# Low parts of six input weight blocks in the first tile: made on VectorE, or by ScalarE and an accumulating DMA

## The chip, the cores and the metric

The kernel runs on one core of a Trainium2 chip. The metric is the device time of one execution in microseconds (us), the median of several runs. Five engines have instruction streams of their own: TensorE (PE; PEld are its weight loads), VectorE (DVE), ScalarE (ACT), GpSimd (POOL) and SyncE (SP, which only issues DMAs). They meet at semaphores, and within one engine the instructions go in the order of the program.

## The reference, cut to what matters

Inputs are float32. Attention in chunks of 64 gives `x` (4608 tokens by 512), and two feed-forward layers follow:

```
h = x @ w_in                      # 512 -> 2048
x = (h * cos(h)) @ w_out          # 2048 -> 512
a, b = x @ w1, x @ w2             # 512 -> 1024 each
out = ((a * b) @ w3) @ w_out2     # 1024 -> 1024 -> 512
```

## The kernel before, in words

**Two-part products.** TensorE multiplies a rounded format (`fp32r`). To keep float32 accuracy every operand is held as a high part (the value rounded to `fp32r`) and a low part (the value minus its high part). `mm3` (lines 111 to 113) makes each product as three matmuls: high x high, weight high x data low, and, on line 113, weight low x data high. So line 113 is the first to read a weight's low part.

**Tiles and groups.** The tokens go in 9 tiles of 512. For each tile the first layer is done in groups of two blocks of `w_in` (blocks `in 2g` and `in 2g+1`, each 128 x 512) and two of `w_out`. Groups 0 to 4 of every tile come first, the others in a second pass. In the first tile a group's work on TensorE is: `stepP` (24 matmuls for one half of the group's hidden values, the first 12 with block `in 2g`, the next 12 with `in 2g+1`), a piece of attention for the next tile, `stepQ` (24 matmuls for the other half), then `x2_mm` of the group before (24 matmuls into `acc`), and more attention. Between them ScalarE and VectorE form `h * cos(h)`.

**Conversion of weights.** The weights come in as 64-bit words and are turned into float32 on the chip, in the first tile, while it is computed. `conv_tick` moves a pipeline by one block: `conv_c` makes the high part `w` of the oldest block (ScalarE, line 189), `conv_b` finishes the next block's float32 value `cw` (VectorE, line 144) and, for an input block, stores it to DRAM, `conv_a` starts the one after (ScalarE line 136, VectorE lines 137 and 138), and then the low part of the oldest block is made. Twenty blocks go through, in the order in 0, in 1, out 0, out 1, in 2, in 3, out 2, ... A hand-written string of letters per group sets the order of all work, and a `v` in it is one tick; there are four in a group, so that each group converts the two output blocks of its own and the two input blocks of the next group. The input blocks are the last two ticks, shortly ahead of the group that reads them.

**Two ways to a low part.** For the input blocks and the output blocks 0 and 1 it is one VectorE subtraction (line 215). For the output blocks 2 to 9 ScalarE writes the negative of the value's rounded part into the low half (line 212), and a DMA that GpSimd issues (line 213) adds the float32 value to it. Those blocks are read by `x2_mm` only, in the next group.

**Where `cw` lives.** A rotating set of three buffers, except for every second of the output blocks 2 to 9, which have halves of weight slot 24.

Of the kernel before, what the change touches and what calls it, by code (L numbers as in the profile page):

```python
# [12 lines left out]
U32 = mybir.dt.uint32  # L13
# [4 lines left out]
P = 128  # L18
NT = 4608
TT = 512  # L20
# [37 lines left out]
def chunk_attention_two_ffn(  # L58
# [15 lines left out]
    wpool = ctx.enter_context(tc.tile_pool(name="wpool", bufs=1))  # L74
# [26 lines left out]
    def f32(ap):  # L101
        return ap.bitcast(F32)
# [10 lines left out]
        nc.tensor.matmul(ps, a[1], b[0], start=False, stop=last)  # L113


    W, raws, halfway, more = {}, {}, {}, []
    src = {"in": w_in, "out": w_out, "w1": w1, "w2": w2, "wo2": wo2, "w3": w3t}

    def load_w(key):
        n = cq.index(key) if key in cq else 0  # L120
        t = (wpool.tile([P, TT, 2], U32, tag=f"w{20 + n % 5}", name="raw") if n >= 5 and n % 5 < 2
             else wk.tile([P, TT, 2], U32, tag="stage", name="raw", bufs=3))
        nc.sync.dma_start(out=t, in_=src[key[0]][key[1]].bitcast(U32).rearrange("p (t w) -> p t w", w=2))
        raws[key] = t

    def conv_a(key):

        raw = raws[key]
        lo, hi = raw[:, :, 0], raw[:, :, 1]
        if key[0] == "out" and key[1] > 1 and key[1] % 2 == 0:  # L130
            if not more:
                more.append(wpool.tile([P, 2, TT], U32, tag=f"w{NSLOT - 1}", name="cw2"))
            m = more[0][:, key[1] // 2 % 2]
        else:
            m = wk.tile([P, TT], U32, tag="cw", name="cw", bufs=3)
        nc.scalar.activation(lo.bitcast(I32), lo, AF.Copy, scale=2.0 ** -29)
        nc.vector.tensor_scalar(m, hi, 3, 0x3FFFFFFF, op0=ALU.logical_shift_left, op1=ALU.bitwise_and)
        nc.vector.scalar_tensor_tensor(m, hi, 0xC0000000, m, op0=ALU.bitwise_and, op1=ALU.bitwise_or)
        halfway[key] = m

    def conv_b(key):

        m = halfway[key].bitcast(I32)
        nc.vector.tensor_tensor(out=m, in0=m, in1=raws.pop(key)[:, :, 0].bitcast(I32), op=ALU.add)
        if key[0] == "in":
            nc.sync.dma_start(out=wr[key[1] // 2][:, key[1] % 2], in_=m.bitcast(F32))
# [3 lines left out]
    def free(owners, n):  # L150
        return sum(o in gone for o in owners) >= n
# [32 lines left out]
    def conv_c(key):  # L184

        pair, second = pair_of(key)
        m = halfway.pop(key).bitcast(F32)
        t = new_w((pair, second) if pair else key)
        nc.scalar.activation(t[:, 0], m, AF.Copy)
        return t, m  # L190
# [4 lines left out]
    def conv_tick():  # L195

        last = None
        if cat[3] < cat[2]:
            if not free(slots, 1):
                return False  # L200
            last = *conv_c(cq[cat[3]]), cq[cat[3]]
            cat[3] += 1
        if cat[2] < cat[1]:
            conv_b(cq[cat[2]])
            cat[2] += 1
        if cat[1] < cat[0]:
            conv_a(cq[cat[1]])
            cat[1] += 1
        if last:
            t, w, key = last  # L210
            if key[0] == "out" and key[1] > 1:
                nc.scalar.activation(t[:, 1], w, AF.Copy, scale=-1.0)
                nc.gpsimd.dma_start(out=f32(t[:, 1]), in_=w, accum_op=ALU.add)
            else:
                nc.vector.tensor_tensor(out=t[:, 1], in0=w, in1=f32(t[:, 0]), op=ALU.subtract)  # L215
        while cat[0] < min(len(cq), cat[1] + (4 if cat[1] > 2 else 2)):
            load_w(cq[cat[0]])
            cat[0] += 1
        return True
# [31 lines left out]
    def need(*keys):  # L251
        while not all(key in W for key in keys):
            assert (pump() if cat[3] == len(cq) else conv_tick()), keys
# [838 lines left out]
    with tc.manual_schedule():  # L1092
        load_qk(0)
        load_qk(1)
        for g in range(GA):
            cq.extend((nm, 2 * g + e) for nm in ("in", "out") for e in range(2))
        load_qk(2)
        conv_tick()
        make_identity(nc, ident)
        nc.vector.memset(half_pi, math.pi / 2)  # L1100
# [6 lines left out]
        for tok in START.split():  # L1107
            if tok == "x":
                conv_tick()
            elif tok == "o":  # L1110
                x_op(plain.pop(0))
            else:
                att_tok(tok, True)
# [20 lines left out]
        for i in range(NG):  # L1134
# [20 lines left out]
            ps, n, g = groups[i]  # L1155
# [203 lines left out]
```

## Time and profile before

| | us |
|---|---|
| median of 3 runs (lowest to highest) | 1459.29 (1458.56 to 1462.25) |
| the profiled execution | 1460.69 |
| its span, first to last instruction | 1458.6 |
| TensorE busy in the span | 1421.1 (97%) |
| VectorE busy | 1200.1 (82%) |
| ScalarE busy | 717.5 (49%) |
| GpSimd busy | 201.1 (14%) |

Busy times overlap, since the engines work side by side. The difference between the execution's time and its span, 2.1 us, lies before the first and after the last instruction of the program. A time in a row is counted from the start of the span.

### The profile page before, as it was taken

To read this page: it belongs to the slowest core of one execution; us is meant where nothing else is said; L and a number is where in the kernel's file an instruction comes from. 1 tells how busy PE (TensorE), PEld (TensorE's weight loads), DVE (VectorE), ACT (ScalarE), POOL (GpSimd) and SP (SyncE) were. 2 spreads that over 40 slices of the span, in tenths; PEclk is the share of its full clock that TensorE was granted. 3 is DMA by queue.
4 is the path that set the end of the run, shared out by engine and by line. 5 is a ranking of instruction groups with operands and counts; after the bars stand their busy time and mean duration, and the time that the engine had idled before them with its cause. 6 is when DMAs were issued, how large, how long until landed. Compare 5 with 4: busy or idle time off the path is not lost.

```text
span 1458.6 us, 27380 instructions
## 1 busy us (share of the span) xinstructions
PE 1421.1 (97%) x10572; PEld 1261.2 (86%) x10572; DVE 1200.1 (82%) x1995; ACT 717.5 (49%) x1201; POOL 201.1 (14%) x151
## 2 busy tenths in 40 slices
PE   5899999999999999999999999999999999999998
PEld 5788888888888888988888888998898888889888
DVE  7989899899988887777778787676797888788777
ACT  4877677777777764444445544231132123123122
POOL 0102112222222222222212222120000000000000
PEclk9999999999999999999999999999999999999999
DMA  8966656566565629989989985586665755856643
GB/s 280 262 189 202 219 154 237 190 214 229 193 236 174 211 95 334 366 303 334 308 306 345 351 310 179 187 319 248 236 220 186 280 196 172 321 173 213 232 145 116
DMA packets 151329, 345.21 MB, mean 237 GB/s; under 512 B 15264, under 2 KB 52896, under 8 KB 150048
## 3 DMA queue, kind: packets, MB, share of 16 engines
q1 hardware_dynamic: 150048, 341.37, 67.9%
q0 software_dynamic: 1152, 2.10, 0.8%
q8 instruction: 84, 1.38, 0.4%
q14 instruction: 45, 0.37, 0.1%
HBM read 240.91 MB, written 100.40 MB: 234 GB/s over the span
## 4 chain that ended last, share of the span: by engine, by line
PE 59%; DVE 1%; DMA 1%; ACT 1%; POOL 1%; issue 0%; SPq 0%; DVEq 0%; POOLq 0%; ACTq 0%
PE ps_hh L111 8%; PE ps_hh L112 8%; PE ps_hh L113 8%; PE acc L112 7%; PE acc L113 7%; PE acc L111 7%; PE ps_aa L111 5%; PE ps_aa L112 5%; PE ps_aa L113 5%; POOL g L630 1%; DVE x2a L659 1%; DMA sd<-spare 0%; DMA raw<-in_w_dram 0%; DMA wfd<-wfo 0%; ACT T L106 0%
## 5 line engine op out<-in xcount | busy, mean ns | idle before, releaser
L630 POOL TENSOR_TENSOR g<-t,g 128x512 fp32r<-128x512 f32 x134 | 185.0, 1401 | 645.4 <-ACT g L629 611.6
L111 PE MATMUL acc<-g,w 128*128 128x512 f32 x576 | 228.1, 396 | 0.0
L112 PE MATMUL acc<-g,w 128*128 128x512 f32 x576 | 227.0, 394 | 0.6 <-POOL g L630 0.5
L113 PE MATMUL acc<-g,w 128*128 128x512 f32 x576 | 224.9, 390 | 0.0
L862 ACT ACTIVATE phl<-w 128x512 fp32r<-128x512 f32 x66 | 41.3, 631 | 292.0 <-DVE w L1053 242.1
L113 PE MATMUL ps_hh<-T,w 128*128 128x256 f32 (+1 forms) x616 | 181.9, 295 | 1.6 <-DVE w L215 1.6
L111 PE MATMUL ps_hh<-T,w 128*128 128x256 f32 (+1 forms) x616 | 182.0, 295 | 0.0
L112 PE MATMUL ps_hh<-T,w 128*128 128x256 f32 (+1 forms) x616 | 181.8, 295 | 0.0
L112 PEld LDWEIGHTS acc<-g,w 128*128 128x128 f32 x576 | 108.6, 188 | 23.7 <-POOL g L630 3.8
L113 PEld LDWEIGHTS acc<-g,w 128*128 128x128 f32 x576 | 108.3, 188 | 23.0
L111 PEld LDWEIGHTS acc<-g,w 128*128 128x128 f32 x576 | 108.7, 189 | 19.8
L113 PEld LDWEIGHTS ps_hh<-T,w 128*128 128x128 f32 x616 | 118.4, 192 | 4.8 <-DVE w L215 2.3
L111 PE MATMUL ps_hh<-B,w 128*128 128x256 f32 (+1 forms) x396 | 120.0, 303 | 1.2 <-DVE d L561 0.6
L111 PEld LDWEIGHTS ps_hh<-T,w 128*128 128x128 f32 x616 | 118.5, 192 | 2.8
L112 PEld LDWEIGHTS ps_hh<-T,w 128*128 128x128 f32 x616 | 118.5, 192 | 2.5
L112 PE MATMUL ps_hh<-B,w 128*128 128x256 f32 (+1 forms) x396 | 116.2, 293 | 0.0
L113 PE MATMUL ps_hh<-B,w 128*128 128x256 f32 (+1 forms) x396 | 116.0, 293 | 0.0
L617 ACT ACTIVATE t<-t,half_pi 128x512 f32<-128x512 f32 x144 | 98.4, 714 | 1.2
L629 ACT ACTIVATE g<-t 128x512 fp32r<-128x512 f32 x144 | 85.6, 629 | 13.5 <-DVE t L621 11.8
L607 ACT ACTIVATE t<-d 128x512 int32<-128x512 f32 x62 | 39.2, 632 | 105.1 <-DVE d L561 104.6
L111 PEld LDWEIGHTS ps_hh<-B,w 128*128 128x128 f32 x396 | 76.3, 193 | 6.8 <-PE acc L113 1.0
L549 DVE TENSOR_TENSOR d<-x,ps_hh 128x512 f32<-128x512 f32 x70 | 47.9, 684 | 39.3 <-ACT g L629 25.0
(304 smaller groups left out, 3774.0 us busy)
## 6 DMA issues: line engine op xcount, KB each, us to landing
w<-sd SPq DMA_DIRECT2D x159, 512.0 KB, 5.7
sd<-raw SPq DMA_DIRECT2D x104, 256.0 KB, 4.3
wset<-twd SPq DMA_DIRECT2D x26, 512.0 KB, 3.9
s<-sd SPq DMA_DIRECT2D x43, 256.0 KB, 5.7
wset<-wfd SPq DMA_DIRECT2D x42, 256.0 KB, 4.2
qk<-in_q_dram SPq DMA_DIRECT2D x36, 256.0 KB, 4.0
qk<-in_k_dram SPq DMA_DIRECT2D x36, 256.0 KB, 4.1
x2a<-x2o SPq DMA_DIRECT2D x36, 256.0 KB, 3.2
```

Source lines behind the costliest of these rows:

```text
L111: nc.tensor.matmul(ps, a[0], b[0], start=first, stop=False)
L112: nc.tensor.matmul(ps, a[0], b[1], start=False, stop=False)
L113: nc.tensor.matmul(ps, a[1], b[0], start=False, stop=last)
L549: nc.vector.tensor_tensor(out=two(self.d), in0=self.x1.unsqueeze(1).to_broadcast([P, 2, 256]), in1=two(p26), op=ALU.add)
L607: nc.scalar.activation(t.bitcast(I32), h, AF.Copy, scale=INV2PI, bias=0.25)
L617: nc.scalar.activation(t, t, AF.Sin, scale=TWO_PI, bias=half_pi)
L629: nc.scalar.activation(hi, r, AF.Copy)
L630: (nc.vector if i < GA else nc.gpsimd).tensor_tensor(out=lo, in0=r, in1=f32(hi), op=ALU.subtract)
L659: nc.vector.tensor_tensor(out=t, in0=t, in1=acc[c], op=ALU.add)
L862: nc.scalar.activation(put[kind, f][0], plane(*SRC[kind], f), AF.Copy)
```

## The change

The low parts of the input blocks in 4 to in 9, those of groups 2, 3 and 4, are made as those of the output blocks 2 to 9 are: ScalarE's negative, then an accumulating DMA. Their `cw` values leave the rotating three buffers for halves of the weight slots 22 and 23.

```diff
@@ conv_a
+        elif key[0] == "in" and key[1] > 3:
+            n = 22 + key[1] // 2 % 2
+            if n not in more_in:
+                more_in[n] = wpool.tile([P, 2, TT], U32, tag=f"w{n}", name="cw3")
+            m = more_in[n][:, key[1] % 2]
         else:
             m = wk.tile([P, TT], U32, tag="cw", name="cw", bufs=3)
@@ conv_tick
             t, w, key = last
-            if key[0] == "out" and key[1] > 1:
+            if key[1] > {"in": 3, "out": 1}[key[0]]:
                 nc.scalar.activation(t[:, 1], w, AF.Copy, scale=-1.0)
                 nc.gpsimd.dma_start(out=f32(t[:, 1]), in_=w, accum_op=ALU.add)
             else:
                 nc.vector.tensor_tensor(out=t[:, 1], in0=w, in1=f32(t[:, 0]), op=ALU.subtract)
```

All other instructions of ScalarE, VectorE, TensorE and SyncE keep their order. The line numbers of the changed kernel are higher by five behind `conv_a`'s new lines.

On TensorE, at the start of group 2's `stepP` (`ps_hh` is its PSUM bank, `B_172`, `B_173` and `T_175` are parts of the data, `w` the weights), the program before waits for VectorE's semaphore at the third and at the fifteenth matmul:

```order
272 L111 MATMUL ps_hh<-B_172,w 128x256 [waits DVE_49,PE_49]
273 L112 MATMUL ps_hh<-B_172,w 128x256
274 L113 MATMUL ps_hh<-B_172,w 128x256 [waits DVE_49]
...
284 L111 MATMUL ps_hh<-T_175,w 128x256 [waits Activation_49]
285 L112 MATMUL ps_hh<-T_175,w 128x256
286 L113 MATMUL ps_hh<-T_175,w 128x256 [waits DVE_49]
287 L111 MATMUL ps_hh<-T_175,w 128x256
```

The same place in the changed program:

```order
272 L111 MATMUL ps_hh<-B_172,w 128x256 [waits DVE_49,PE_49]
273 L112 MATMUL ps_hh<-B_172,w 128x256
274 L113 MATMUL ps_hh<-B_172,w 128x256 [waits DMASW2_49]
...
284 L111 MATMUL ps_hh<-T_175,w 128x256 [waits Activation_49]
285 L112 MATMUL ps_hh<-T_175,w 128x256
286 L113 MATMUL ps_hh<-T_175,w 128x256 [waits DMASW3_49]
287 L111 MATMUL ps_hh<-T_175,w 128x256
```

The matmuls stand where they stood; the two line-113 matmuls now wait for the completion of GpSimd's DMAs (`DMASW`), and so do those of groups 3 and 4.

On ScalarE, at the end of group 1 (the ticks that convert in 4 and in 5; `ex`/`pt` and `xf` are attention's tiles, `g` the hidden values), before:

```order
57 L136 ACTIVATE raw<-raw 128x512
58 L447 ACTIVATE pt<-ps_at 128x512
59 L189 ACTIVATE w<-cw 128x512
60 L136 ACTIVATE raw<-raw 128x512
61 L469 ACTIVATE xf<-ps_at 128x2x4x64
62 L629 ACTIVATE g<-t 128x2x256 x2
```

and in the changed program:

```order
57 L141 ACTIVATE raw<-raw 128x512
58 L217 ACTIVATE w<-cw_700 128x512
59 L452 ACTIVATE pt<-ps_at 128x512
60 L194 ACTIVATE w<-cw_700 128x512
61 L141 ACTIVATE raw<-raw 128x512
62 L217 ACTIVATE w<-cw_700 128x512
63 L474 ACTIVATE xf<-ps_at 128x2x4x64
64 L634 ACTIVATE g<-t 128x2x256 x2
```

One activation (line 212 before, 217 now) is added behind each tick's line 136 (now 141); GpSimd's DMA of the block follows it.

## Rows read from the trace of the kernel before

**Rows 1.** The page: span and busy time of each engine.

```profile
span 1458.6 us, 27380 instructions
PE 1421.1 (97%) x10572; PEld 1261.2 (86%) x10572; DVE 1200.1 (82%) x1995; ACT 717.5 (49%) x1201; POOL 201.1 (14%) x151
```

**Rows 2.** Windows: busy time of each engine in a stretch, then granted clock, DMA.

```profile
core 0: us, PE busy (x) PEld busy (x) DVE busy (x) ACT busy (x) POOL busy (x), PEclk, DMA share, GB/s
57.00:91.00 34.00, 30.58 (x366) 27.27 (x367) 33.42 (x61) 30.66 (x50) 4.10 (x5) 1.00 0.80 220
110.00:1458.00 1348.00, 1333.67 (x9591) 1183.61 (x9589) 1107.06 (x1818) 638.27 (x1070) 193.08 (x137) 1.00 0.68 236
```

**Rows 3.** Waits of PE by line, whole span: total us, times, longest.

```profile
PE ps_at L459 <- ACT pt L447: 2.7, 4, 0.7
PE ps_hh L113 <- DVE w L215: 1.6, 3, 0.6
```

**Rows 4.** Timeline of PE: `stepP` of group 2, then where groups 3, 4 wait.

```profile
58.49 0.39 PE L111 MATMUL ps_hh<-B,w 128*128 128x256 f32 x1
...
58.83 0.28 PE L113 MATMUL ps_hh<-B,w 128*128 128x256 f32 x1
58.95 0.28 PE L111 MATMUL ps_hh<-B,w 128*128 128x256 f32 x1
...
60.87 0.39 PE L113 MATMUL ps_hh<-T,w 128*128 128x256 f32 x1 [0.45 <-DVE w L215]
...
75.43 0.39 PE L113 MATMUL ps_hh<-T,w 128*128 128x256 f32 x1 [0.61 <-DVE w L215]
...
89.98 0.39 PE L113 MATMUL ps_hh<-T,w 128*128 128x256 f32 x1 [0.59 <-DVE w L215]
```

**Rows 5.** Line 215 on DVE, groups 2 to 4 (57 to 92 us).

```profile
L215 DVE TENSOR_TENSOR w<-cw,w x6: 681/684/686, 57.3 to 89.2; 128x512 fp32r<-128x512 f32 x6
```

**Rows 6.** Timeline of ACT: ticks of in 4, in 5, in 7 and in 9.

```profile
55.15 0.61 ACT L189 ACTIVATE w<-cw 128x512 fp32r<-128x512 f32 x1
55.67 0.69 ACT L136 ACTIVATE raw<-raw 128x512 int32<-128x512 uint32 x1
...
57.77 0.69 ACT L136 ACTIVATE raw<-raw 128x512 int32<-128x512 uint32 x1
...
72.16 0.69 ACT L136 ACTIVATE raw<-raw 128x512 int32<-128x512 uint32 x1
...
86.73 0.69 ACT L136 ACTIVATE raw<-raw 128x512 int32<-128x512 uint32 x1
```

**Rows 7.** Timeline of ACT and POOL: a tick of an output block, out 4.

```profile
60.69 0.66 ACT L136 ACTIVATE raw<-raw 128x512 int32<-128x512 uint32 x1
61.24 0.62 ACT L212 ACTIVATE w<-cw 128x512 fp32r<-128x512 f32 x1
...
62.16 0.90 POOL L213 DMA_DIRECT2D w<-cw  x1 [10.82 <-DVE g L630]
```

**Rows 8.** Line 213, the eight accumulating DMAs: issue on POOL, time to landing.

```profile
L213 POOL DMA_DIRECT2D w<-cw x8: 859/862/1050, 46.7 to 93.4; - x8
DMA to landing us min/median/max: 4.3/7.2/11.4
```

**Rows 9.** Timeline of PE around its longest wait, 35.6 to 39.7 us.

```profile
39.72 0.66 PE L444 MATMUL ps_at<-ident,ex 128*128 128x128 f32 x4 [4.14 <-DVE ex L437]
...
43.35 0.41 PE L112 MATMUL ps_hh<-B,w 128*128 128x256 f32 x1
43.57 0.41 PE L113 MATMUL ps_hh<-B,w 128*128 128x256 f32 x1
```

**Rows 10.** Windows around that wait (columns as in rows 2).

```profile
35.50:39.50 4.00, 0.08 (x1) 0.00 (x0) 3.86 (x9) 3.97 (x7) 0.00 (x0) 1.00 0.98 365
40.00:40.50 0.50, 0.38 (x4) 0.14 (x2) 0.50 (x2) 0.09 (x1) 0.00 (x0) 0.80 0.45 180
40.50:47.00 6.50, 5.94 (x83) 5.82 (x84) 6.43 (x12) 4.87 (x9) 0.32 (x1) 0.50 0.73 220
47.50:50.50 3.00, 3.00 (x27) 3.00 (x26) 2.71 (x5) 2.52 (x5) 0.26 (x2) 1.00 1.11 228
```

**Rows 11.** DMA queues, 0 to 130 us: packets, MB, time of 16 engines.

```profile
q0 software_dynamic: 1152, 2.10, 9.2%
```

More of the change, by code (lines that the diff above doesn't have):

```diff
@@ L113, in mm3 @@
         nc.tensor.matmul(ps, a[1], b[0], start=False, stop=last)
-    W, raws, halfway, more = {}, {}, {}, []
+    W, raws, halfway, more, more_in = {}, {}, {}, [], {}
     src = {"in": w_in, "out": w_out, "w1": w1, "w2": w2, "wo2": wo2, "w3": w3t}
```

## The prediction

> **What bounds the kernel now.** The page comes first: TensorE is busy in 1421 of 1458.6 us [rows 1]. What delays TensorE is therefore paid in full unless a later idle stretch takes it up, and the windows show hardly any: from 110 us on it is busy in 1333.67 of 1348 us [rows 2]. The change touches only the ticks of in 4 to in 9, so the second look goes to groups 2 to 4, 57 to 91 us. There VectorE is the fullest engine, 33.42 of 34 us, ScalarE has 30.66 and TensorE 30.58 [rows 2]. The third view, TensorE's waits, says what VectorE's fullness costs: 1.6 us in three waits of line 113 for the subtraction on line 215, and the timeline puts one in each of the three groups, at 60.87, 75.43 and 89.98 us [rows 3, 4]. That is the fifteenth matmul of `stepP`, the first that reads the low part of the group's second block. The other waits of these groups, 0.7 us each for attention's line 447 [rows 3], are not touched.
>
> **What is removed.** Six subtractions on VectorE of 0.684 us [rows 5], 4.1 us in all. VectorE off the path is worth nothing; what TensorE can win is what it waited for them, 1.6 us.
>
> **What is added on ScalarE and GpSimd.** Six negatives of about 0.62 us [rows 7], 3.7 us. They stand behind line 136 in their ticks, so they hold up what follows by half a microsecond each: line 447 is waiting for TensorE at that point anyway, and the activations behind the second tick (469 and 629) feed matmuls that stand behind the 48 of `stepP` and `stepQ`. I cost them at nothing; without that cover the price would be the 3.7 us. The six issues on GpSimd take 0.86 to 1.05 us each [rows 8]; GpSimd had been idle 10.8 us before its next DMA at this place [rows 7]. Six more accumulating DMAs move the data: eight of them took 9.2% of the 16 engines' 130 us, 1.5 us each [rows 11], a small load beside the rest. Slots 22 and 23, where `cw` now lives, are needed as weight slots only in the second tile, behind 110 us; nothing on the path asks for them earlier.
>
> **What is moved onto the path.** The matmuls that waited for VectorE now wait for a DMA to land. When is each issued? In an output block's tick the negative starts 0.55 us after line 136, and the DMA starts on GpSimd 0.92 us after the negative (60.69, 61.24, 62.16) [rows 7], together 1.47 us. Behind line 136 of in 4, in 5, in 7 and in 9 (55.67, 57.77, 72.16, 86.73) [rows 6] that makes DMA starts at 57.14, 59.24, 73.63 and 88.20 us. And when are the parts needed? That of in 4 at the third matmul, 58.83, and those of in 5, in 7 and in 9 at 60.87, 75.43 and 89.98 [rows 4]. From start to need there are 1.69, 1.63, 1.80 and 1.78 us. The same kind of DMA, same size and same tiles, took 4.3 to 11.4 us to land, 7.2 in the median of eight [rows 8]. It was hidden there because an output block is read a group later; here nothing lies between. Line 113 waits for landing minus 1.75 us:
>
> - shortest landing: 4.3 - 1.75 = 2.6 us a group, 7.7 us in three;
> - median: 7.2 - 1.75 = 5.45 us, 16.4 us in three;
> - longest: 11.4 - 1.75 = 9.65 us, 29 us in three.
>
> Most of the wait falls on the third matmul (in 4), the rest, if any, on the fifteenth, since the second DMA starts 2.1 us behind the first and the matmuls from one to the other took 60.87 - 58.83 = 2.04 us [rows 4]. The waits of 1.6 us that go away are already in the sum, because the starts are compared with the times at which TensorE went on. Does the stall pass to the next group in full? The tick of a group's second block hangs on line 447, that is on TensorE's transposes late in the group before, so it moves with TensorE, and the next stall is as long again. I take the median.
>
> **The clock.** Once before, TensorE stood still for 4.14 us [rows 9]. The granted clock was still 1.00 in the idle stretch, fell just behind it and was 0.50 (1.2 of 2.4 GHz) from 40.5 to 47 us, then 1.00 again [rows 10]. Matmuls of 256 columns started 0.22 us apart in it [rows 9], against 0.12 at full clock [rows 4]. A stall of 5.45 us is longer than that one, so I expect the same behind it: half clock for some 6.5 us after the fall. Part of this is covered, as the twelve matmuls between the two waits have time anyway. Counting from a fall 4.5 us after the stall began (63.4) to 69.9, with matmuls resumed at 64.3: twelve at 0.22 us bring the fifteenth to 66.9 instead of 66.4 us, and the 3.0 us that remain at half clock lose 1.3 us. That is 1.8 us a group. The bounds are zero (no fall, as a short stall may leave it) and 6.5 x (1 - 0.12/0.22) = 3 us. I take 1.2 a group, 3.6 us in all, for two falls out of three.
>
> **The sum.** 16.4 + 3.6 = +20 us on the profiled execution: 1460.7 becomes 1480.7 us. That execution was 1.4 us above the median of 1459.3, so the median becomes 1479 us. The ends are +7.7 (shortest landings, no fall) and 29 + 9 = +38 us.
>
> **Rivals.** (1) *VectorE's relief wins and the DMA is hidden.* For it: VectorE is full in 33.42 of 34 us [rows 2] and TensorE waits for it in each group. It decides if the DMAs land within 1.75 us of their start. The result would be 1.6 us less, 1457.7, within what can be measured. Against it: not one of eight landed in under 4.3 us. Chance 2%.
>
> (2) *The landing is short because these DMAs stay on the chip.* At 2.6 us from start to landing, the stall is 0.85 us a group, 2.6 us in all, no clock falls, and the time is 1462 us: no change that a measurement of this kernel can tell, which takes about 0.3%, 4.4 us. For it: no single cause of the long landings is visible, so other traffic may explain them, and a stalled TensorE holds back some of that traffic. Against it: the six blocks meet the same loads, one per tick, as the eight that were measured. Chance 6%. The Trainium skill, "DMA: Bandwidth & Descriptors", section "Anatomy of one DMA — SWDGE (gpsimd) path", fits a DMA of this kind as 2.0 us plus its bytes over 436 GB/s; by that, as an estimate, 256 KB take 2.6 us, which is this rival's case. The trace does not agree, with 4.3 us at the least [rows 8].
>
> (3) *The landings are at the long end.* GpSimd's DMAs of one group now come in a row, in 4, in 5, then out 4, and the three share their queue. From landings of about 9.5 us on, the stall is 7.8 us and the clock falls each time for the full price: 3 x (7.8 + 2.4) = +30 us, 1490 us. For it: three of the eight come near it, as a median of 7.2 and an end of 11.4 show [rows 8]. Against it: each DMA is only 1.5 us of the engines' time. Chance 8%. The Trainium skill, "SBUF — State Buffer", in its box on the trap that DVE blocks DMA, says that GpSimd cannot write a DMA's descriptors while VectorE runs an operation on both ports. Here VectorE is busy 98% of the time, which would make this rival likelier, but the issues took 0.86 to 1.05 us, an even figure [rows 8], and in the new stalls VectorE would have pauses.
>
> **Chances and range.** The forecast, landings of about 4.3 to 9.5 us and a time of 1467 to 1490, has 84%, and the rivals 2, 6 and 8%. I give 1467 to 1490 as the range: below it lie rivals 1 and 2, above it rival 3. Rivals 1 and 2 end within 0.3%, 8%, of which I leave one point to a gain above all that TensorE waited for here, whose source I have not seen: faster by over 0.3% 1%, within it 7%, slower 92%.
>
> **What would show it.** In the changed kernel's waits, line 113 waits for the DMA on line 218 in groups 2, 3 and 4, six times at most, 14 to 22 us in total, and the row for the subtraction (now line 220) is gone. The landing of the six DMAs is 4.3 to 9.5 us. Behind each stall the granted clock is 0.50 for several microseconds. From group 4's end on, all is later by the same amount, and VectorE, without its six subtractions, shows idle time in 57 to 110 us. I am wrong if the DMAs start much earlier than 1.5 us behind line 141, if they land within 3 us, or if TensorE makes up the loss later: the last would show as waits before that are gone behind 110 us, of which there are only 14 us in all [rows 2].

## The result and the profile after

The changed kernel takes 1479.22 us in the median of 4 runs (1476.11 to 1482.35), the kernel before 1459.34 us beside it (1458.56 to 1462.25). The ratio is 1.0133, with a 95% interval of 1.012 to 1.0146: slower by 20 us. The profiled execution took 1478.13 us, its span is 17.7 us longer than that of [rows 1], and this is what the views below account for.

The page of the changed kernel, span and busy time of each engine:

```profile
span 1476.3 us, 27396 instructions
PE 1427.6 (97%) x10572; PEld 1266.0 (86%) x10572; DVE 1198.2 (81%) x1989; ACT 721.5 (49%) x1207; POOL 206.0 (14%) x157
```

VectorE has lost its six subtractions, ScalarE and GpSimd have six instructions more each. TensorE has as many matmuls as in [rows 1], but they took 6.5 us longer: a sign of a lower clock somewhere. Its waits, whole span (total us, times, longest):

```profile
PE ps_hh L113 <- DMA w<-cw: 14.0, 6, 3.9
PE ps_at L464 <- ACT pt L452: 2.8, 4, 0.7
```

The row for the subtraction, 1.6 us in [rows 3], is gone; line 113 now waits 14.0 us for the new DMAs, three times on the matmuls that waited for VectorE before and three times on matmuls that did not wait. The wait for attention (line 464, 459 before) is what it was. Where they stand, in TensorE's timeline:

```profile
57.54 0.39 PE L111 MATMUL ps_hh<-B,w 128*128 128x256 f32 x1
...
61.92 0.54 PE L113 MATMUL ps_hh<-B,w 128*128 128x256 f32 x1 [3.88 <-DMA w<-cw]
...
62.48 0.41 PE L112 MATMUL ps_hh<-B,w 128*128 128x256 f32 x1
62.69 0.41 PE L113 MATMUL ps_hh<-B,w 128*128 128x256 f32 x1
...
65.88 0.39 PE L113 MATMUL ps_hh<-T,w 128*128 128x256 f32 x1 [1.07 <-DMA w<-cw]
...
77.92 0.39 PE L111 MATMUL ps_hh<-B,w 128*128 128x256 f32 x1
...
81.37 0.38 PE L113 MATMUL ps_hh<-B,w 128*128 128x256 f32 x1 [2.94 <-DMA w<-cw]
...
85.68 0.58 PE L113 MATMUL ps_hh<-T,w 128*128 128x256 f32 x1 [2.25 <-DMA w<-cw]
...
99.28 0.39 PE L111 MATMUL ps_hh<-B,w 128*128 128x256 f32 x1
...
100.89 0.39 PE L113 MATMUL ps_hh<-B,w 128*128 128x256 f32 x1 [1.11 <-DMA w<-cw]
...
105.31 0.39 PE L113 MATMUL ps_hh<-T,w 128*128 128x256 f32 x1 [2.72 <-DMA w<-cw]
...
110.98 0.40 PE L111 MATMUL acc<-g,w 128*128 128x512 f32 x1
```

The lines at 57.54, 77.92 and 99.28 us are the first matmuls of `stepP` in groups 2, 3 and 4, the last line is the first of group 4's `x2_mm`. In the kernel before, that of group 2 stands in [rows 4]; the other three are:

```profile
72.89 0.39 PE L111 MATMUL ps_hh<-B,w 128*128 128x256 f32 x1
...
87.46 0.39 PE L111 MATMUL ps_hh<-B,w 128*128 128x256 f32 x1
...
94.15 0.40 PE L111 MATMUL acc<-g,w 128*128 128x512 f32 x1
```

Two waits in each of groups 2, 3 and 4: on the third matmul of `stepP` (in 4, in 6, in 8) and on the fifteenth (in 5, in 7, in 9). The fifteenth matmuls stood at 60.87, 75.43 and 89.98 us in [rows 4]; they are later by 5.01, 10.25 and 15.33 us. `stepP` of group 2 began 0.95 us earlier than in [rows 4]. That is not the change's doing: the granted clock behind the long wait of group 0 was 1.00 again from 45 us on, where [rows 10] has 0.50 until 47 us. Behind the waits, windows (busy time of each engine, then the granted clock, the DMA share and GB/s):

```profile
core 0: us, PE busy (x) PEld busy (x) DVE busy (x) ACT busy (x) POOL busy (x), PEclk, DMA share, GB/s
61.95:65.30 3.35, 2.86 (x12) 2.56 (x12) 0.07 (x1) 0.00 (x0) 0.34 (x1) 0.51 1.07 292
82.50:89.20 6.70, 4.45 (x21) 4.15 (x20) 0.35 (x1) 0.98 (x2) 0.18 (x1) 0.50 0.81 201
106.35:109.45 3.10, 3.10 (x17) 3.10 (x16) 0.69 (x1) 1.64 (x3) 0.51 (x1) 0.50 1.01 326
57.00:115.00 58.00, 42.63 (x390) 37.84 (x380) 34.05 (x61) 37.24 (x63) 9.53 (x12) 0.88 0.79 214
110.00:1458.00 1348.00, 1337.18 (x9578) 1184.80 (x9577) 1108.55 (x1820) 647.34 (x1082) 193.06 (x137) 1.00 0.68 236
```

In each group the clock falls to 0.50 (1.2 of 2.4 GHz), for 3.1 to 3.4 us in groups 2 and 4 and for 6.7 us in group 3, whose second wait lies inside the stretch; matmuls start 0.21 to 0.22 us apart there (62.48, 62.69). The three stretches hold 2.86 + 4.45 + 3.10 = 10.4 us of busy TensorE; at 0.12 in place of 0.22 us a matmul [rows 4, 9] they would have taken 5.7, so 4.7 us are lost in them.

**The account.** Where `stepP` of group 2 began 0.95 us early and the span ends 17.7 us late, 18.6 us came in between, 0.84 us of it spread over the rest of the program and 17.8 in groups 2 to 4. By what TensorE did in them, waits make 14.0 - 1.6 = 12.4 us, and the other 5.4 are matmuls at the lower clock: 4.7 us in the stretches of 0.50, the rest on their edges.

By cause the split is another. A group's second DMA starts before the clock falls (at 58.32 us against 62.0 in group 2), and the fifteenth matmul waits for it in every group. A matmul that is slower between the two waits therefore only shortens the second wait. What the DMAs cost is how much later the fifteenth matmul comes within its group: 5.01 + 0.95 = 5.96 us in group 2, 10.25 - 5.03 = 5.22 in group 3 and 15.33 - 11.82 = 3.51 in group 4, together 14.7. (5.03 and 11.82 are the delays of the `stepP` starts above.) What the clock costs is what is added behind the fifteenth matmul: 0.02, 1.57 and 1.50 us, together 3.1.

TensorE's 1337.18 us in the last window, against 1333.67 of the same 1348 [rows 2], only say that the window now begins later in the program.

### The profile page after: what moved, and what is told of

Read it like the earlier page. It is cut to its first block, busy times and chain, and to the rows that moved or that the text cites. A ratio compares the mean times of both kernels' runs of the same rounds, so it can differ in the third digit from the quotient of the medians.

```text
span 1476.3 us, 27396 instructions
## 1 busy us (share of the span) xinstructions
PE 1427.6 (97%) x10572; PEld 1266.0 (86%) x10572; DVE 1198.2 (81%) x1989; ACT 721.5 (49%) x1207; POOL 206.0 (14%) x157
## 4 chain that ended last, share of the span: by engine, by line
PE 56%; DVE 3%; DMA 2%; ACT 1%; POOL 1%; issue 0%; SPq 0%; DVEq 0%; POOLq 0%; ACTq 0%
PE ps_hh L111 7%; PE ps_hh L112 7%; PE ps_hh L113 7%; PE acc L112 6%; PE acc L113 6%; PE acc L111 6%; PE ps_aa L111 5%; PE ps_aa L112 5%; PE ps_aa L113 5%; DMA raw<-in_w_dram 1%; DVE x2a L664 1%; POOL g L635 1%; DMA T<-xs6T 1%; DMA B<-xs3B 1%; DMA B<-xs5B 1%
## 5 line engine op out<-in xcount | busy, mean ns | idle before, releaser
L113 PE MATMUL ps_hh<-B,w 128*128 128x256 f32 (+1 forms) x396 | 117.6, 297 | 7.9 <-DMA w<-cw 7.9
L111 PE MATMUL ps_hh<-B,w 128*128 128x256 f32 (+1 forms) x396 | 121.0, 306 | 0.7 <-ACT xf L470 0.5
L112 PE MATMUL ps_hh<-B,w 128*128 128x256 f32 (+1 forms) x396 | 117.4, 297 | 0.0
L113 PEld LDWEIGHTS ps_hh<-B,w 128*128 128x128 f32 x396 | 77.8, 196 | 9.8 <-DMA w<-cw 8.6
L111 PEld LDWEIGHTS ps_hh<-B,w 128*128 128x128 f32 x396 | 77.5, 196 | 6.1 <-ACT xf L470 0.7
```

The costliest lines, as they stand in the source:

```text
L111: nc.tensor.matmul(ps, a[0], b[0], start=first, stop=False)
L112: nc.tensor.matmul(ps, a[0], b[1], start=False, stop=False)
```

## Experiments

**1. The buffers alone.** The new slots of `cw` stay, the low parts are VectorE's again:

```diff
-            if key[1] > {"in": 3, "out": 1}[key[0]]:
+            if key[0] == "out" and key[1] > 1:
```

> The float32 values of in 4 to in 9 stay in the weight slots 22 and 23, but their low parts are VectorE's subtraction again, without negative and without DMA. Theory (all of the loss is TensorE's wait for the six accumulating DMAs and the clock that falls behind it): the loss is gone, about 1459 us, 1457 to 1461, and line 113 waits some 1.6 us for VectorE as before. Rival (the new home of the values costs the time: loads into slots 22 and 23 or the order of releases): it stays above 1470 us.

Measured: 1460.07 us against 1459.6, ratio 0.9998 (0.999 to 1.0007). TensorE's waits have the old row back:

```profile
PE ps_hh L113 <- DVE w L220: 1.7, 3, 0.6
```

The move to slots 22 and 23 costs nothing that these runs can tell, 0.07% at most.

**2. The negatives without the DMA.** The low parts of in 4 to in 9 stay the negatives alone; the block is not added:

```diff
                 nc.scalar.activation(t[:, 1], w, AF.Copy, scale=-1.0)
-                nc.gpsimd.dma_start(out=f32(t[:, 1]), in_=w, accum_op=ALU.add)
+                if key[0] == "out":
+                    nc.gpsimd.dma_start(out=f32(t[:, 1]), in_=w, accum_op=ALU.add)
```

> The six negatives stay on ScalarE, the six accumulating DMAs are left out, so the low parts of in 4 to in 9 are the negatives of the high parts and the output is not the reference's. Theory: line 113 waits for ScalarE's negative, which ends within 1.0 us of need, so hardly at all; the time is that of before less the 1.6 us that TensorE waited for VectorE, 1456.5 to 1459.5 us. Rival (the 3.7 us of negatives on a full ScalarE delay line 452 and what follows): 1461 us or more, up to 1463.

Measured: 1458.6 us, ratio 0.9992 (0.9984 to 1.0001), and no wait of line 113 in groups 2 to 4. ScalarE's six negatives are covered, as the prediction costed them. The whole loss hangs on the DMA. It also bounds VectorE's relief: with every wait for the subtraction gone, at most 0.16% came back.

**3 and 4. Inputs converted ahead of the outputs.** The list of blocks takes the next group's input blocks before the group's own output blocks, so that a group lies between a DMA and its reader. Number 3 is the changed kernel with this order, number 4 the kernel before with it, as a control:

```diff
+        cq.extend(("in", e) for e in range(2))
         for g in range(GA):
-            cq.extend((nm, 2 * g + e) for nm in ("in", "out") for e in range(2))
+            cq.extend(("in", 2 * g + 2 + e) for e in range(2) if g < GA - 1)
+            cq.extend(("out", 2 * g + e) for e in range(2))
```

> The changed kernel with another order of conversion: in each group the next group's two input blocks go ahead of the group's own two output blocks, so their DMAs start two ticks, some 7 to 10 us, earlier, and the output blocks' DMAs two ticks later. Theory (only the distance from start to need is wrong): line 113 in stepP no longer waits for a DMA, no fall of the clock, and the time is that of before or a little less, 1456 to 1461 us; the output blocks' DMAs start some 8 us before their need and may cost up to 2 us. Rival (six more accumulating DMAs cost time wherever they stand, by contention in their queue or on the DMA engines): above 1465 us.

> Control for the run with the inputs first: the kernel before, with that order of conversion and VectorE's subtraction for all input blocks. Theory: the 1.6 us of waits of line 113 for VectorE go, nothing else changes, 1457 to 1459.5 us. If the time is the same as that of the run with the DMAs, VectorE's six subtractions are worth nothing where they do not stand right ahead of their need; if it is longer by 1 to 4 us, the relief of VectorE is worth that much.

Measured: number 3 1461.08 us, ratio 1.0009 (1.0 to 1.0018), at the upper end of its expectation; number 4 1463.91 us, 1.0029 (1.0018 to 1.0039), which misses its expectation. In number 3 the waits of `stepP` for the DMA are gone, though the 14 DMAs land after 4.0 to 9.9 us (median 7.5), no sooner than before. The order has a price of its own, in group 0, and the timeline of number 3 (DVE and PE) shows it:

```profile
37.30 0.43 DVE L142 TENSOR_SCALAR cw<-raw 128x512 uint32<-128x512 uint32 x1 [2.62 <-DMA wr<-cw]
...
41.47 1.12 PE L449 MATMUL ps_at<-ident,ex 128*128 128x128 f32 x4 [6.38 <-DVE ex L442]
```

Four input blocks in a row use up the three rotating `cw` buffers; VectorE waits 2.62 us until SyncE has stored one, and TensorE's wait for attention grows from 4.14 [rows 9] to 6.38 us. Number 4 has 6.24 us there, and two new waits of 2.7 us in all for attention's values on line 437, since VectorE is busy in 47.38 of the 50 us from 45 to 95, against 44.45 in number 3. With this order the six subtractions less are worth the difference of the two medians, 2.8 us; their intervals just touch.

**5. The same order from group 1 on**, which leaves group 0 as it was:

```diff
-        for g in range(GA):
-            cq.extend((nm, 2 * g + e) for nm in ("in", "out") for e in range(2))
+        for n in (0, -1, 1, 2, -2, 3, -3, 4, -4, -5):
+            cq.extend(("in" if n >= 0 else "out", 2 * abs(n) - 2 * (n < 0) + e) for e in range(2))
```

> The changed kernel with the inputs first from group 1 on, and group 0 in the old order (out 0, out 1, in 2, in 3). In the run with the inputs first everywhere TensorE's long wait in group 0 grew from 4.1 to 6.4 us, as VectorE waited 2.6 us for the store of in 2's value out of one of the three rotating buffers; behind it TensorE won back 2.1 us by the end of group 4, while the control with VectorE's subtraction lost another 2.4 us by then. Theory (the DMAs are hidden by two ticks' distance, and VectorE's relief then counts): no such wait in group 0, no wait of line 113 in stepP, 1456 to 1458.5 us, 1 to 3 us under the kernel before. Rival (the relief is worth nothing, the 2.1 us were only a recovery from group 0's delay): 1459 to 1461 us.

Measured: 1458.04 us against 1459.18, ratio 0.9991 (0.9983 to 1.0). What is left of line 113's waits for the DMA:

```profile
PE acc L113 <- DMA w<-cw: 0.5, 1, 0.5
```

and the landing of its 14 DMAs:

```profile
DMA to landing us min/median/max: 3.4/7.7/9.9
```

The whole 20 us are gone with DMAs that land later than in the changed kernel (median 6.8). So it is the place of the DMA just ahead of its reader that costs, not the DMA. This version has the lowest median of all here, 1.1 us under the kernel before, at the edge of what its runs can tell. In its trace TensorE gains 1.1 us on the kernel before in groups 2 to 4.

**6. A plain copy in place of the accumulation.** The low parts are then copies of the block:

```diff
-                nc.gpsimd.dma_start(out=f32(t[:, 1]), in_=w, accum_op=ALU.add)
+                if key[0] == "in":
+                    nc.gpsimd.dma_start(out=f32(t[:, 1]), in_=w)
+                else:
+                    nc.gpsimd.dma_start(out=f32(t[:, 1]), in_=w, accum_op=ALU.add)
```

> The changed kernel with a plain copy of the value in place of the accumulation in the six input blocks' DMAs (GpSimd issues them as before), so their low parts are the full value and the output is not the reference's. It tells what makes a landing of 3.4 to 8.8 us. If the accumulation does (a read and a write of the destination for each element), the copy lands in under 3.5 us, line 113 waits under 6 us in all and the time is about 1466 us. If issue, queue and other traffic do, it lands as the accumulating ones do, 3.4 to 8 us, line 113 waits 11 to 14 us and the time stays at 1475 to 1480 us. I hold the second likelier, as the same GpSimd queue and the same busy engines serve both.

Measured: 1475.87 us, ratio 1.011 (1.0096 to 1.0124). The six copies (ns of an issue on POOL, first and last start), and their landing:

```profile
L219 POOL DMA_DIRECT2D w<-cw x6: 552/560/570, 55.9 to 98.5; - x6
DMA to landing us min/median/max: 2.3/5.2/7.3
```

and TensorE's wait for them:

```profile
PE ps_hh L113 <- DMA w<-cw: 11.1, 6, 4.4
```

A copy is issued in 0.56 instead of 0.86 us and waited for 2.9 us less in six. The six land after 5.1 us in the mean against 5.6, so most of the landing is not the adding. Where no load stands ahead, in 8, the copy lands after 2.3 us against 3.4, so there the adding may be a third of it; that is one DMA in one execution of each.

**7. Work in the waits.** Matmuls with a zero operand, which add nothing, stand ahead of the waiting ones in groups 2 to 4 (20 ahead of the third, 10 ahead of the fifteenth). The edit in `mm3`, without the lines that pass `fill` and make `zero`:

```diff
         nc.tensor.matmul(ps, a[0], b[1], start=False, stop=False)
+        for _ in range(fill):
+            nc.tensor.matmul(ps[0:32], zero, b[0], start=False, stop=False)
         nc.tensor.matmul(ps, a[1], b[0], start=False, stop=last)
```

> The changed kernel with 30 more matmuls in stepP of groups 2, 3 and 4 (20 ahead of the third and 10 ahead of the fifteenth matmul), which add zeros (32 columns of zero weights by 256) and fill the waits by some 2.4 and 1.2 us. Theory (of the 17.8 us some 12.4 are waits and 5.4 the slower matmuls behind them): the granted clock stays at 1.00 or falls for a shorter time, and the time drops by 3 to 6 us to 1473 to 1476 us, although work is added. Rival (the slower matmuls are hidden in the next wait anyway, so only the landings count): no gain, 1478 to 1481 us. If the clock falls as before in spite of the filling, the run tells nothing.

Measured: 1476.28 us, ratio 1.0121 (1.0105 to 1.0136). The window that in the changed kernel shows a clock of 0.88:

```profile
57.00:115.00 58.00, 51.29 (x508) 45.79 (x509) 36.14 (x64) 38.15 (x65) 10.32 (x12) 0.97 0.80 219
```

With TensorE kept busy the clock held in groups 2 and 4 and fell in group 3 alone. In the trace this ties the fall to the pause. It also bears out the split of the account: the second DMAs of the three pairs land after 19.9 us in sum (19.7 in the changed kernel), the clock is 1.00 behind every fifteenth matmul, nothing is lost there, and groups 2 to 4 cost 15.3 us in place of 17.8. In time it is inconclusive: 1476.28 us just misses the expected 1473 to 1476, and the interval overlaps that of the changed kernel.

**8. One group's pair alone**, in 4 and in 5:

```diff
-            if key[1] > {"in": 3, "out": 1}[key[0]]:
+            if key in (("in", 4), ("in", 5)) or key[0] == "out" and key[1] > 1:
```

> Only in 4 and in 5 (group 2) get the negative and the accumulating DMA; in 6 to in 9 have VectorE's subtraction again. Theory (each group pays its own stall and nothing makes it up): about a third of the loss, +6 us, 1465 us, 1463 to 1468, with TensorE behind by 6.0 us at the end of group 2 and by the same at the end of the span. Rivals: later groups make up for it, as VectorE and ScalarE get ahead in the stall (under 1462 us); or the loss is one of the three groups together, by the longer queue of DMAs (under 1463 us for one pair).

Measured: 1464.24 us, +5.1 us, ratio 1.0035 (1.0022 to 1.0047), which is 3.2 to 6.9 us. TensorE's waits of line 113:

```profile
PE ps_hh L113 <- DMA w<-cw: 4.5, 2, 3.5
...
PE ps_hh L113 <- DVE w L220: 0.6, 1, 0.6
```

One group costs a quarter of the whole by the medians; the third that equal shares would make lies within the interval. In the trace TensorE begins group 2 1.3 us early and is 5.5 us late at its end, and 0.6 us come back as one of the two other groups' waits for VectorE vanished. From there to 740 us it stays 4.9 to 5.0 us late, so the groups behind make up nothing. The span ends 3.5 us late, because a stretch at half clock that the kernel before has behind a wait of 1.7 us does not occur in this execution:

```profile
900.50:903.80 3.30, 3.30 (x14) 3.11 (x15) 1.59 (x4) 0.63 (x1) 0.00 (x0) 0.50 0.97 279
```

**9 and 10. What makes the landing long.** The six DMAs of the changed kernel landed after 5.7, 7.5, 4.7, 6.9, 3.4 and 5.2 us (in 4 to in 9; windows 56 to 60, 76 to 80 and 97 to 101 us, one pair each):

```profile
DMA to landing us min/median/max: 5.7/6.6/7.5
DMA to landing us min/median/max: 4.7/5.8/6.9
DMA to landing us min/median/max: 3.4/4.3/5.2
```

Ahead of each DMA of in 4 to in 7 SyncE starts one load of 512 KB for an output block; ahead of in 8 and in 9 none is left to load. (The expectation of number 10 speaks of two such loads ahead of in 4 and of in 6; the second starts behind that DMA, ahead of the next.) The 256 KB store of a `cw` stands ahead of in 4, in 6 and in 8 alike. Changed kernel, timeline of SP and POOL:

```profile
55.78 0.39 SPq L123 DMA_DIRECT2D raw<-in_w_out_dram  x1
...
56.21 0.86 POOL L218 DMA_DIRECT2D w<-cw  x1 [5.82 <-ACT w L217]
...
57.62 0.33 SPq L123 DMA_DIRECT2D raw<-in_w_out_dram  x1
...
58.32 0.86 POOL L218 DMA_DIRECT2D w<-cw  x1 [1.25 <-ACT w L217]
...
97.41 0.86 POOL L218 DMA_DIRECT2D w<-cw  x1 [5.84 <-ACT w L217]
```

and its DMA queues, from 56.4 to 58.4 us (between the issue of in 4 and its data), then from 97.8 to 98.6 and from 98.6 to 100.4 (the same for in 8, and its data); q1 is SyncE's, q0 GpSimd's; packets, MB, share of the 16 engines' time:

```profile
q1 hardware_dynamic: 205, 0.56, 90.4%
q0 software_dynamic: 2, 0.00, 0.6%
...
q1 hardware_dynamic: 67, 0.10, 35.5%
...
q0 software_dynamic: 143, 0.26, 85.9%
q1 hardware_dynamic: 5, 0.01, 0.8%
```

For in 4 the engines are 90% taken by SyncE's packets for 2 us before the first of GpSimd's data move; for in 8 they are mostly free, and its 0.26 MB pass in 1.8 us. Number 9 holds the loads of the input ticks back behind the pair, number 10 adds two transfers of that size in the tick of in 8 (copies that nothing reads; the lines that make their target are left out below). The first starts 0.46 us ahead of the DMA, the second 0.15 us behind its start:

```diff
+        held_back = last and key[0] == "in" and key[1] > 3
-        while cat[0] < min(len(cq), cat[1] + (4 if cat[1] > 2 else 2)):
+        while not held_back and cat[0] < min(len(cq), cat[1] + (4 if cat[1] > 2 else 2)):
```

```diff
+        if last and key == ("in", 8):
+            for e in range(2):
+                nc.sync.dma_start(out=again[e], in_=w_out[e].bitcast(U32).rearrange("p (t w) -> p t w", w=2))
```

> The changed kernel, with the raw weight loads of SyncE (512 KB each) that the ticks of in 4 to in 9 issue held back to the next output tick, behind the pair's accumulating DMAs. In the changed kernel two such loads start 0.43 us ahead of the DMA of in 4 and of in 6 (55.78 and 76.16 against 56.21 and 76.60 us), whose landings are 5.7 and 4.7 us (7.5 and 6.9 for the second of each pair); no load stands ahead of in 8, which lands in 3.4 us. Theory A, the landing is lengthened by the packets that SyncE's queue has put before the 16 DMA engines: the landings of in 4 to in 7 fall to about 3.5 us for the first and 4 to 5 for the second of a pair, line 113 waits 8 to 10 us in place of 14.0, and the time is about 1471 to 1475 us, if the held-back raw loads do not come late themselves (which would show as ScalarE waiting for raw). Theory B, the landing is the DMA's own (its queue on GpSimd, its descriptors, its completion): landings 4.7 to 7.5 as before, line 113 waits 14 us, and the time is 1479 us.

> The changed kernel, with two added transfers of 512 KB on SyncE (copies of two weight blocks from DRAM to DRAM, which nothing reads) in the tick of in 8, where the changed kernel has no raw loads left and the accumulating DMA lands in 3.4 us (in 9: 5.2). Theory A, SyncE's packets lengthen the landing: in 8 lands in 5 to 6 us, as in 4 and in 6 do behind two such loads, in 9 in 6 to 7.5, group 4 waits about 2 to 3 us more and the time is 1481 to 1483 us. Theory B, the landing is the DMA's own: 3.4 and 5.2 us again, and 1479 us.

Measured, number 9: 1472.67 us, ratio 1.0085 (1.0064 to 1.0106); landings 3.7, 5.6, 3.7, 5.3, 3.3 and 4.5 us, in pairs:

```profile
DMA to landing us min/median/max: 3.7/4.6/5.6
DMA to landing us min/median/max: 3.7/4.5/5.3
DMA to landing us min/median/max: 3.3/3.9/4.5
```

Its waits of line 113:

```profile
PE ps_hh L113 <- DMA w<-cw: 10.0, 6, 2.7
```

Number 10: 1481.29 us, 1.0136 (1.011 to 1.0163); in 8 lands after 8.8 and in 9 after 8.2 us, and TensorE's waits (line 114 here) are

```profile
PE ps_hh L114 <- DMA w<-cw: 16.4, 5, 6.8
```

The two changes, of opposite sign, moved the landing as theory A said (that of number 10 further than the 5 to 6 us expected). In time number 9 is clearly below the changed kernel; number 10's median is as expected, but its interval contains the changed kernel's, so its time shows nothing. In its trace group 4 costs 9.0 us against 5.0. VectorE's load does not explain the landings: it was busy in 3.26 of the 3.68 us of number 9's in 4, in 5.20 of the changed kernel's 5.67, and in 4.33 of the 8.84 us of number 10's in 8. With no load ahead of it, the first DMA of a pair lands in 3.3 to 3.7 us in every group. The second takes 1.2 to 1.9 us more even then: it starts 2.1 to 3.2 us behind the first and shares its queue and the engines with what SyncE has sent meanwhile. How that part divides was not tried.

## Why the prediction held

**The mechanism** held as it stood. Line 113 waits six times, in groups 2 to 4, 14.0 us in all (14 to 22 forecast), the subtraction's row is gone, the clock is 0.50 behind the waits, and nothing is made up behind 110 us. The 14.0 us lie at the lower end of what was forecast. That 1479 and 1479.2 us agree so closely is luck: the runs lie between 1476.1 and 1482.4, and the two profiled executions, for which the sum was made, differ by 17.4 us and not by 20.

**When the DMA starts.** "Together 1.47 us" behind ScalarE's first step of the tick: in the changed kernel 1.48 and 1.50 us (timeline of ACT and, in the fence of experiments 9 and 10, POOL):

```profile
54.73 0.67 ACT L141 ACTIVATE raw<-raw 128x512 int32<-128x512 uint32 x1
55.30 0.62 ACT L217 ACTIVATE w<-cw 128x512 fp32r<-128x512 f32 x1
...
56.82 0.69 ACT L141 ACTIVATE raw<-raw 128x512 int32<-128x512 uint32 x1
```

**The landing** is the term that was mis-sized. The prediction took the median of [rows 8], 7.2 us, for both DMAs of a pair. Its rule, landing minus start to need, holds for the second DMA, which sets a group's delay: landings of 7.5, 6.9 and 5.2 us, less 1.6 to 1.7, are the 5.96, 5.22 and 3.51 us of the account. So the term was 14.7 us where 16.4 stood. "The next stall is as long again" failed with group 4, where no load was left. Experiments 9 and 10 show why: the landing is not a property of this DMA alone but also of what SyncE's queue has sent ahead of it, and that differs from place to place. Rival 2 had named other traffic as a possible cause. But even with the loads out of the way no landing came down to its 2.6 us; the best was 3.3. As for the Trainium skill, "DMA: Bandwidth & Descriptors", section "Anatomy of one DMA — SWDGE (gpsimd) path": by its fit, as an estimate, 256 KB take 2.6 us, and no accumulating DMA of this kernel came below 3.3, while one plain copy (experiment 6) took 2.3.

**The split between the two waits.** "Most of the wait falls on the third matmul": the third has 3.88 + 2.94 + 1.11 = 7.9 us and the fifteenth 1.07 + 2.25 + 2.72 = 6.0. The second DMA of a pair lands 1.8 to 2.2 us slower than the first, where the prediction let both take the median. Whether that is rival 3's worry, DMAs in a row that hinder each other, was not tried. None of the six landed as late as the 9.5 us that it was priced with.

**The clock** was priced at 1.2 us a group, 3.6 us in all, for two falls out of three. It fell in all three, and in group 2 the whole stretch at 0.50 lay between the two waits, where the prediction had said that the matmuls "have time anyway"; it cost 1.57 and 1.50 us in the other two. So the size, 3.1 us, came out for another reason than the one given. With it, 14.7 + 3.1 = 17.8 us stand where 16.4 + 3.6 = 20 was forecast.

**What was costed at nothing** cost nothing that can be told: the slots (experiment 1), the negatives (experiment 2). VectorE's relief went unused in the changed kernel: in 57 to 110 us it waits 18.1 us for ScalarE, which waits for the stalled matmuls. Of its waits in that stretch:

```profile
DVE t L617 <- ACT t L612: 18.1, 5, 6.5
```

Rival 1 asked for a landing within 1.75 us; none came near it. But its idea is right where the DMA has time: experiment 5 keeps the relief and hides the landing.

## What to carry to other kernels

Work taken from a full engine is worth only what the bound engine waited for it, here 1.6 us, and a DMA in its place has to be issued earlier than its reader by its whole landing time: count from issue to need before anything else. The landing of a small DMA is read at its own place, with what the other queues have sent just before it, and not taken from the median of the same DMA elsewhere. If the DMA is wanted, move its place in the order (experiment 5), not its speed.

## What the runs showed of the hardware

The same accumulating DMA of 256 KB, from SBUF to SBUF, took 3.3 to 3.7 us to land as the first of a pair with no load of SyncE's just ahead of it, 4.7 to 5.7 with one load of 512 KB started 0.4 us before it, and 8.8 with two copies of that size from DRAM to DRAM started around it; one queue's small transfer is held up by another's large ones. A plain copy was issued by GpSimd in 0.56 us, an accumulating one in 0.86. Two waits of 1.1 to 3.9 us in a group, with twelve matmuls between them, brought the clock down to 0.50 in each group. A single short wait did so in some places and not in others: the kernel before waits 1.7 us for VectorE at 866.4 us and again at 900.3 us, and the clock fell behind the second alone; in the changed kernel it fell behind the first, at 884.0 us, alone.
